# Value products of 64 keys in quarters of the TensorE array, in two PSUM banks, inside the second product

## The chip, the cores and the metric

The kernel runs on one core of a Trainium2 chip. The time is what the device takes for one execution, in microseconds (us). Three runs of the kernel before took 995.18, 995.64 and 997.73 us; their median is 995.64. One further execution was profiled.

## The reference

Sliding-window attention (8 batches, 8 heads, 576 positions, head size 64, window 128, a slope per head) feeds a two-layer network with a squared relu.

```python
scores = scale * np.matmul(q, k.transpose(0, 1, 3, 2))
bias = slopes[:, None, None] * (-np.abs(rel).astype(np.float32))[None, :, :]
mask = (rel >= 0) & (rel < window)
scores = np.where(mask, scores + bias[None], -1000000000.0)
scores = scores - np.max(scores, axis=-1, keepdims=True)
attn = np.exp(scores)
attn = attn / (np.sum(attn, axis=-1, keepdims=True) + 1e-09)
attn_out = np.matmul(attn, v)
x = attn_out.transpose(0, 2, 1, 3).reshape(B * S, H * D)      # 4608 x 512
h = np.maximum(x @ w_in, 0.0)                                 # w_in 512 x 2048
out = h * h @ w_out                                           # w_out 2048 x 512
```

## The kernel before

The 4608 rows are cut into 9 chunks of 512 columns (the data lies transposed: features on partitions, rows along the free axis). For each chunk the network runs 16 steps f. A **first product** (`gemm1`, L169) multiplies 128 columns of w_in with the chunk's attention output: 12 products of 512 columns into the PSUM bank g, four input tiles times three high and low parts. ScalarE's relu (L178) reads g, VectorE squares (L184), ScalarE casts the high part hh (L186), VectorE takes the low part hl (L188). A **second product** (`gemm2`, L199) multiplies w_out with hh and hl of two steps earlier: four output banks acc, three products each. The program alternates first and second products; each is a half step t, first products at even t, second products at odd t.

Attention for the next chunk is put between these products. A chunk has four pairs of heads; a pair has two **segments** of 256 rows, sg 0 and sg 1, and both together form a `Couple`. Every eight half steps there is a **visit** (part 0 in the main loop). It does the value products of the couple before (`both`, which calls `mix`, L335) into the bank at, reads at out to xu (ScalarE's cast L359, VectorE's subtraction L360), loads the q, k and v of the next couple (SP), and makes the score products of a new couple (`Couple.scores`, L414), which write two banks s and the bank g. The scores of segment 1 share g between the two heads j; a GpSimd no-operation lets the second head start only when the first is done there. Then ScalarE copies the scores out (`base`, L441 and L448), VectorE puts the part of the earlier keys in (`fold`, L460 and L464), VectorE and ScalarE make the softmax (L276, L283), GpSimd divides by the sum (`norm`, L294). Three and five half steps behind the visit a `middle` stands ahead of a first product, once for each segment: TensorE transposes the weights (`turn`, L302), ScalarE copies them (L309), GpSimd splits them into `prev` and `own`, the keys of the block before and of the same block, with zeros where a key does not belong (L312, L318).

`mix` multiplies, for each segment, i = 0, 1 and both heads j, 128 keys of `prev` and 128 keys of `own` with v: products of 128 columns in half of the array each (128 rows by 64 columns), accumulated in the bank at.

Each name of a PSUM tile (g, at) has one buffer: g goes from the first product to its relu, and at a visit to the scores and ScalarE's copies of them, and then to the next first product. The order on TensorE is that of the program text in the main loop; on the other engines a scheduler places the instructions by a simulated time line. The start of the program (about 145 us) is ordered by a planner; the change touches it at segment 16 alone.

Of the kernel before, what the change touches and what calls it, by code (L numbers as in the profile page):

```python
# [33 lines left out]
LATER = [("z", 7)]  # L34
RING = lambda k: 55 + 10.5 * (k - 8)
CONV = lambda f: 36 + 6 * f
FIRST = 35
SYNC = mybir.DependencyInfo(mybir.DependencyClass.Sync, mybir.DependencyReason.DATA)
CST = 256 + 128 * H
ENGINES = {e: getattr(mybir.EngineType, e) for e in ("PE", "DVE", "Activation", "Pool", "SP")}  # L40
# [6 lines left out]
class Kern:  # L47
    def __init__(self, ctx, tc, qkd, vd, w1d, w2d, cstd, outd):
        self.tc, self.nc = tc, tc.nc
        self.qkd, self.vd = qkd, vd  # L50
        self.w1d, self.w2d, self.cstd, self.outd = w1d, w2d, cstd, outd
        ep = lambda name, bufs, **kw: ctx.enter_context(tc.tile_pool(name=name, bufs=bufs, **kw))
        self.c = ep("const", 1)
        self.ld = ep("ld", 3)
        self.tp = ep("tp", 3)
        self.pp = ep("pp", 2)
        self.sm = ep("sm", 6)
        self.xu = ep("xu", 8)
        self.hp = ep("hp", 3)
        self.op = ep("op", 4)  # L60
        self.sc = ep("sc", 1, space=PSUM)
        self.at = ep("at", 1, space=PSUM)
        self.g1 = ep("g1", 1, space=PSUM)
        self.ac = ep("ac", 4, space=PSUM)
        self.cst = self.c.tile([128, CST], F32, name="cst")
        self.ident = self.cst[:, 0:128]
        self.mask = self.cst[:, 128:192].bitcast(I32)
        self.never = self.cst[:, 192:256]
        self.raw, self.w = [None] * NF, [None] * NF
        self.nc.alloc_sbuf_tensor("arena", [128, NF * 2048], F32)  # L70
        self.arena = self.nc.sbuf_base - NF * 8192
        self.x, self.qk, self.v, self.h, self.segs = {}, {}, {}, {}, {}
        at = lambda slot, name, shape: self.nc.alloc_sbuf_tensor_at(name, shape, F32, offset=self.arena + slot * 4096).ap()
        self.wide = [at(2 * (NF - 3), "wide", [128, H, 256])[:, 2 * p : 2 * p + 2] for p in range(NP)]
        self.room_t = [at(2 * (NF - 5) + n, f"tw{n}", [128, 4, 256]) for n in range(4)]
        self.start_banks = [self.ac.tile([128, 512], F32, name="acc") for _ in range(4)]
# [111 lines left out]
        nc.vector.tensor_tensor(hl, r, hh.bitcast(F32), op=ALU.subtract)  # L188

    def gemm2(self, c, f):  # L190
        nc = self.nc
        hh, hl = self.h.pop((c, f))
        if f == 0:
            self.acc = self.start_banks if c == 0 else [self.ac.tile([128, 512], F32, name="acc") for _ in range(4)]
        wh, wl = self.w[f][:, 1, :, 1], self.w[f][:, 1, :, 0]
        for m in range(4):
            ms = slice(m * 128, m * 128 + 128)
            for i, (w, h) in enumerate(((wh, hh), (wh, hl), (wl, hh))):
                nc.tensor.matmul(  # L199
                    self.acc[m], w[:, ms], h, start=(f == 0 and i == 0), stop=(f == NF - 1 and i == 2)  # L200
                )
            if f == NF - 1:
                o = self.op.tile([128, 512], F32, name="o")
                out = self.outd[m * 128 : m * 128 + 128, 512 * c : 512 * c + 512]
                if c == NCH - 1 and m == 3:
                    nc.scalar.copy(o[:, 0:256], self.acc[m][:, 0:256])
                    nc.vector.tensor_copy(o[:, 256:512], self.acc[m][:, 256:512])
                    nc.sync.dma_start(out[:, 0:256], o[:, 0:256])
                    nc.scalar.dma_start(out[:, 256:512], o[:, 256:512])
                    continue  # L210
                (nc.scalar.copy if m % 2 else nc.vector.tensor_copy)(o, self.acc[m])
                nc.sync.dma_start(out, o)


class Segment:
# [133 lines left out]

    def both(self, other):
        K = self.K
        X = K.at.tile([128, 512], F32, name="at")
        for s in (self, other):
            s.X = X[:, 256 * s.sg : 256 * s.sg + 256]
            s.mix(s.sg == 0)
        u = K.x[self.c, self.p] = K.xu.tile([128, 2, 512], F32R, name="xu")
        self.nc.scalar.copy(u[:, 0], X)  # L359
        self.nc.vector.tensor_tensor(u[:, 1], X, u[:, 0].bitcast(F32), op=ALU.subtract)  # L360

    def soft(self):
        for m in range(4):
# [12 lines left out]
class Couple:  # L376
# [4 lines left out]

    def __init__(self, K, q):
        self.K, self.nc = K, K.nc
        self.both = [Segment(K, 2 * q), Segment(K, 2 * q + 1)]

    def scores(self):
        K, nc = self.K, self.nc
        self.S = K.sc.tile([128, 2, 512], F32, name="s")  # L390
        self.G = K.g1.tile([128, 512], F32, name="g")
        todo = []
        for h in range(2):
            base, extra = (h, h + 1), (2 - 2 * h,)
            for j in range(2):
                first = [(0, i, p) for i in range(2) for p in ([(0, 1, 2)] if h == 0 else [base, extra])]
                shared, rest = ([(1, i, p) for i in range(2)] for p in (base, extra))
                at = 0
                for s, i, part in shared + first + rest if j == 0 else first + rest + shared:
                    blocks = [x for x in part if x >= self.both[s].late.get(2 * i + h, 0)]  # L400
                    if blocks:
                        to, n = self.spot(s, j, i, part == extra), len(blocks)
                        a = 64 * (blocks[0] - part[0])
                        todo.append((at, h, j, s, i, blocks[0], n, to[64 * h : 64 * h + 64, a : a + 64 * n], s == 1 and part == base))
                        at += 64 * n
        done = None
        qk = K.qk[self.both[0].c, self.both[0].p]
        for at, h, j, s, i, a, n, to, shared in sorted(todo, key=lambda y: y[:3]):
            u, r = 4 * s + 2 * i + h, slice(64 * j, 64 * j + 64)
            q0, k0 = 64 * u + 640 * s, 256 + 64 * (u + a)  # L410
            if shared and j == 1 and done:
                turn = nc.gpsimd.nop()
                K.tc.add_manual_dep(turn.ins, done.ins.name, SYNC, reason="one head at a time in the shared bank")
            mm = nc.tensor.matmul(  # L414
                to, qk[r, q0 : q0 + 64], qk[r, k0 : k0 + 64 * n], start=True, stop=True, skip_group_check=True,
            )
            if shared and j == 0:
                done = mm
            elif shared and done:
                K.tc.add_manual_dep(mm.ins, turn.ins.name, SYNC, reason="one head at a time in the shared bank")  # L420
                done = None
# [173 lines left out]
def start(K):  # L595
# [31 lines left out]
    for k in range(18):  # L627
# [19 lines left out]
        else:  # L647
# [6 lines left out]
                P.add(n("e", m), "Activation", 0.4, (n("t", m),) + ((n("e", m - 1),) if m else ()), d + 0.5, do(G.exp, m))  # L654
            P.add(n("r"), "DVE", 0.4, (n("e", 3),), d + 1, G.sums)
            P.add(n("n"), "Pool", 1.05, (n("r"),), d + 1, G.norm)
            if k > 16:
                continue
            P.add(n("z"), "PE", 0.55, (n("n"),) + chain("z"), d + 1, G.turn, ("at", "pp"), "t")
            P.add(n("o"), "Activation", 0.6, (n("z"),), d + 1, G.out, None, "at")  # L660
            P.add(n("p"), "Pool", 0.72, (n("o"),), d + 1.5, G.before)
            P.add(n("m"), "Pool", 0.66, (n("p"),), d + 1.5, G.same)
            if k > 15:
                continue
            P.add(n("x"), "PE", 1.1, (n("m"), ("v", c, p)) + chain("x"), d + 2, G.values, "at", "pp")
            P.add(n("h"), "Activation", 0.4, (n("x"),), d + 2, G.high)
            P.add(n("l"), "DVE", 0.36, (n("h"),), d + 2, G.low, None, "at")
# [26 lines left out]
@with_exitstack  # L694
def tile_attn_moe(ctx: ExitStack, tc: tile.TileContext, *aps):
    K = Kern(ctx, tc, *aps)
    K.const()
    with tc.manual_schedule(engines={ENGINES["PE"]}):
        with tc.manual_schedule(engines={e for n, e in ENGINES.items() if n != "PE"}):
            start(K)  # L700
        pairs = {8: (K.segs[16], K.segs[17])}
        for n in range(NF, NF * NCH + 2):
            for t in (2 * n, 2 * n + 1):
                q, part = divmod(t - FIRST, 8)
                q += 9
                with tc.high_priority(offset=50):
                    if part == 0:
                        if q - 1 in pairs:
                            first, second = pairs.pop(q - 1)
                            first.both(second)  # L710
                        if q + 1 < 4 * NCH:
                            K.load(*divmod(q + 1, 4))
                        if q < 4 * NCH:
                            C = Couple(K, q)
                            C.front()
                            pairs[q] = C.both
                    if part in (3, 5) and q in pairs:
                        pairs[q][part // 4].middle()
                if t % 2 == 0 and n < NF * NCH:
                    for _ in K.gemm1(*divmod(n, NF)):  # L720
                        pass
                if t % 2:
                    K.gemm2(*divmod(n - 2, NF))


def _consts():
# [47 lines left out]
```

## Time and profile before

| what | us |
|---|---|
| median of three runs | 995.64 |
| the profiled execution | 996.04 |
| its span, first to last instruction | 994.2 |
| TensorE busy, all matrix products | 984.2 |
| first product, L169 | 433.9 |
| second product, L199 with hh and with hl | 388.7 and 227.6 |
| value products, L335 into at | 63.8 |

The profile's page gives the busy time of each engine, then the chain of work that ended last, then groups of instructions with their idle time and what ended it. In its rows PE is TensorE's products, PEld its weight loads, DVE is VectorE, ACT ScalarE, POOL GpSimd, SP SyncE. A row of a group reads: line, engine, operation, output<-input, shapes, count, busy time and mean duration. A group's busy time counts the overlap of products in different parts of the array once; rows of the chain show what TensorE spends on a piece from end to end. The kernel's products of fp32 data leave two records each in the trace.

### The profile page before, as it was taken

The page shows a single profiled execution, that of the slowest core. Times are in us where ns is not written, and L with a number is a line of the kernel's source. Part 1 is how long each engine was busy: PE and PEld are TensorE (multiplying, and loading weights), DVE is VectorE, ACT ScalarE, POOL GpSimd, SP SyncE. Part 2 cuts the span into 40 slices and gives each one's busy share as a digit, 9 for nine tenths or more (in the row PEclk, how much of TensorE's full clock was granted, in tenths as well). Part 3 has the DMA queues.
Part 4 walks back from the last instruction along what each step waited for, and adds up shares of the span by engine and source line. Part 5 has one row for each costly group of instructions (what it writes and reads, how often), then busy time and mean ns, then how long its engine had stood idle before and what let it go on. Part 6 is the DMA issues. An engine that isn't in the chain of part 4 may idle for free.

```text
span 994.2 us, 16896 instructions
## 1 busy us (share of the span) xinstructions
PE 984.2 (99%) x6545; PEld 814.1 (82%) x6548; DVE 438.4 (44%) x1269; ACT 453.7 (46%) x1180; POOL 191.8 (19%) x252
## 2 busy tenths in 40 slices
PE   9899999999999999999999999999999999999998
PEld 5678788888888888888888888888888888888886
DVE  6889824444443434344444344333434444422222
ACT  7899744444433444344444343334444444422221
POOL 4132321221112222222212211122222221100000
PEclk9999999999999999999999999999999999999999
DMA  9971202111211002111211121110111110001001
GB/s 350 404 276 53 63 14 80 38 39 38 80 38 39 26 20 73 39 38 38 81 38 38 38 80 38 38 39 19 65 35 39 38 57 1 1 1 43 1 1 42
DMA packets 26943, 61.50 MB, mean 62 GB/s; under 512 B 2928, under 2 KB 4336, under 8 KB 26864
## 3 DMA queue, kind: packets, MB, share of 16 engines
q1 hardware_dynamic: 26432, 59.91, 17.4%
q8 instruction: 51, 0.84, 0.3%
q10 hardware_dynamic: 432, 0.52, 0.2%
q14 instruction: 28, 0.23, 0.1%
HBM read 50.99 MB, written 9.44 MB: 61 GB/s over the span
## 4 chain that ended last, share of the span: by engine, by line
PE 97%; DVE 1%; ACT 1%; issue 0%; POOL 0%; DVEq 0%; POOLq 0%; ACTq 0%
PE acc L199 41%; PE g L169 40%; PE at L335 6%; PE at L302 3%; PE s L414 2%; PE g L414 2%; PE g L105 1%; PE s L239 1%; PE acc L335 1%; PE at L530 0%; PE s L498 0%; PE acc L498 0%; PE acc L533 0%; DVE tw L508 0%; ACT w L155 0%
## 5 line engine op out<-in xcount | busy, mean ns | idle before, releaser
L169 PE MATMUL g<-xu,w 128*128 128x512 f32 x1728 | 433.9, 400 | 2.6 <-ACT r L178 2.6
L199 PE MATMUL acc<-hh,w 128*128 128x512 f32 x1152 | 388.7, 398 | 0.0
L169 PEld LDWEIGHTS g<-xu,w 128*128 128x128 f32 x1728 | 333.3, 196 | 65.3 <-ACT r L178 3.3
L199 PEld LDWEIGHTS acc<-hh,w 128*128 128x128 f32 x1152 | 224.8, 195 | 46.1 <-issue 1.5
L184 DVE TENSOR_TENSOR r<-r 128x512 f32<-128x512 f32 x128 | 88.6, 692 | 342.3 <-ACT r L178 340.4
L199 PE MATMUL acc<-hl,w 128*128 128x512 f32 x576 | 227.6, 395 | 0.0
L178 ACT ACTIVATE r<-g 128x512 f32<-128x512 f32 x144 | 85.5, 594 | 299.5 <-PE g L169 299.2
L188 DVE TENSOR_TENSOR hl<-r,hh 128x512 fp32r<-128x512 f32 x144 | 102.2, 710 | 108.9 <-ACT hh L186 104.7
L186 ACT CAST hh<-r 128x512 fp32r<-128x512 f32 x144 | 89.2, 619 | 95.0 <-DVE r L184 94.5
L199 PEld LDWEIGHTS acc<-hl,w 128*128 128x128 f32 x576 | 112.5, 195 | 20.4
L294 POOL TENSOR_TENSOR t<-t,nm 128x512 f32<-128x512 f32 x64 | 81.1, 1267 | 239.2 <-DVE nm L291 214.2
L283 ACT ACTIVATE t<-t,nm 128x128 f32<-128x128 f32 x256 | 99.5, 390 | 35.2 <-DVE nm L276 35.0
L312 POOL TENSOR_SCALAR_AFFINE_SELECT pp<-pp 128x512 f32<-128x512 f32 x64 | 43.4, 679 | 185.7 <-ACT pp L309 185.6
L335 PEld LDWEIGHTS at<-pp,v 128*64 128x64 f32 x1024 | 55.2, 137 | 12.7 <-issue 12.0
L335 PE MATMUL at<-pp,v 128*64 128x128 f32 x1024 | 63.8, 276 | 0.0
L309 ACT COPY pp<-at 128x512 f32<-128x512 f32 x72 | 42.1, 584 | 45.5 <-PE at L302 44.5
L276 DVE CUSTOM_DVE_ANT_0 t<-t,cst 128x128 f32<-128x128 f32 x256 | 59.2, 293 | 1.0
L450 POOL MEMSET t<- 64x128 f32 (+1 forms) x35 | 8.1, 232 | 236.3 <-PE g L414 235.9
L460 DVE COPY_PREDICATED t<-cst,s 64x256 f32<-64x256 int32 x85 | 37.8, 445 | 32.4 <-ACT t L448 19.1
L283 ACT ACTIVATION_READ_ACCUMULATOR t<-t,nm 128x1 f32 x256 | 48.0, 187 | 0.0
L318 POOL TENSOR_SCALAR_AFFINE_SELECT pp<-pp 128x512 f32<-128x512 f32 x64 | 42.3, 661 | 4.4
L414 PE MATMUL s<-qk 64*64 64x64 f32 (+2 forms) x988 | 40.2, 253 | 0.0
(71 smaller groups left out, 587.4 us busy)
## 6 DMA issues: line engine op xcount, KB each, us to landing
raw<-in_dram SPq DMA_DIRECT2D x32, 512.0 KB, 8.9
qk<-in_dram SPq DMA_DIRECT2D x32, 320.0 KB, 3.5
v<-in_dram SPq DMA_DIRECT2D x32, 320.0 KB, 3.0
qk<-in_dram SPq DMA_DIRECT2D x38, 256.0 KB, 3.8
out_dram<-o SPq DMA_DIRECT2D x35, 256.0 KB, 2.7
v<-in_dram SPq DMA_DIRECT2D x3, 256.0 KB, 5.0
wide<-in_dram SPq DMA_DIRECT2D x3, 256.0 KB, 5.2
qk__200<-in_dram SPq DMA_DIRECT2D x2, 256.0 KB, 5.6
```

The costliest lines, as they stand in the source:

```text
L169: nc.tensor.matmul(g, w[:, cc * 128 : cc * 128 + 128], xs[cc][:, part], start=i == 0, stop=i == 11)
L178: nc.scalar.activation(r, g, AF.Relu)
L184: nc.vector.tensor_tensor(r, r, r, op=ALU.mult)
L186: nc.scalar.copy(hh, r)
L188: nc.vector.tensor_tensor(hl, r, hh.bitcast(F32), op=ALU.subtract)
L199: nc.tensor.matmul(self.acc[m], w[:, ms], h, start=(f == 0 and i == 0), stop=(f == NF - 1 and i == 2))
L276: self.nc.vector.tensor_tensor_reduce(self.t[:, m], self.t[:, m], self.K.nrel(2 * self.p + m // 2), -0.125, BIG, ALU.add, ALU.min, self.nm ...
L283: self.nc.scalar.activation(self.t[:, m], self.t[:, m], AF.Exp, bias=nm[:, m : m + 1], scale=-1.0, accum_out=nm[:, 4 + m : 5 + m],)
L294: self.nc.gpsimd.tensor_tensor(self.t, self.t, self.nm[:, 8:12].unsqueeze(2).to_broadcast([128, 4, 128]), op=ALU.mult)
L312: self.nc.gpsimd.affine_select(self.prev, self.own, pattern=[[0, 4], [-1, 128]], compare_op=ALU.is_gt, fill=0.0, base=0, channel_multiplier=1,
L335: self.nc.tensor.matmul(self.X[r, o : o + 128], v[:, 2 * sg + k, r], src[:, j], start=start and n == 0, stop=n == 3 - self.skip, skip_grou ...
L414: mm = nc.tensor.matmul(to, qk[r, q0 : q0 + 64], qk[r, k0 : k0 + 64 * n], start=True, stop=True, skip_group_check=True,)
```

## The change

`quarters` takes the place of `mix` in a visit. It cuts the 128 keys in halves of 64, each in one row half of the array, and with the two heads j in the two column halves each product uses a quarter. The first half of the keys accumulates in the bank at, the second half in the bank g (a tile of g is made ahead of the values, and the scores of the same visit use it afterwards). In each block half of the queries are left out where the weights are zero, so that half of the products have 64 columns. The two banks are added when they are read out: VectorE copies segment 0's half of g and ScalarE segment 1's to an SBUF tile, VectorE adds at to it, and the cast and the subtraction read the sum. The score products of head j = 1 come first in g, those of j = 0 wait for them. `gemm2` is a generator now, and a visit stands behind the first three of its twelve products. FIRST goes from 35 to 37, so that visits stand a step later against the chunks, and the middle of segment 16 goes from the start to the steady part.

```diff
-FIRST = 35
+FIRST = 37
...
     def gemm2(self, c, f):
+        for _ in self.gemm2_parts(c, f):
+            pass
+
+    def gemm2_parts(self, c, f):
...
+            yield
...
-    def both(self, other):
-        K = self.K
+    def quarters(self, X):
+        K, sg = self.K, self.sg
+        v = K.v[self.c, self.p]
+        own, prev = (a.rearrange("p (j i) c -> p j i c", j=2) for a in (self.own, self.prev))
+        for i in range(2):
+            for full in (True, False):
+                for half in range(2):
+                    src, k = (own, 1) if full == (half == 0) else (prev, 0)
+                    a, e = (0, 128) if full else (64 * half, 64 * half + 64)
+                    r = slice(64 * half, 64 * half + 64)
+                    for j in range(2):
+                        d = slice(64 * j, 64 * j + 64)
+                        self.nc.tensor.matmul(
+                            X[half][d, 128 * i + a : 128 * i + e], v[r, 2 * sg + i + k, d], src[r, j, i, a:e],
+                            start=sg == 0 and i == 0 and full, stop=True, skip_group_check=True,
+                        )
+
+    def both(self, other, G):
+        K, nc = self.K, self.nc
         X = K.at.tile([128, 512], F32, name="at")
+        u = K.x[self.c, self.p] = K.xu.tile([128, 2, 512], F32R, name="xu")
         for s in (self, other):
-            s.X = X[:, 256 * s.sg : 256 * s.sg + 256]
-            s.mix(s.sg == 0)
-        u = K.x[self.c, self.p] = K.xu.tile([128, 2, 512], F32R, name="xu")
-        self.nc.scalar.copy(u[:, 0], X)
-        self.nc.vector.tensor_tensor(u[:, 1], X, u[:, 0].bitcast(F32), op=ALU.subtract)
+            a = 256 * (1 - s.sg)
+            s.X = X[:, 256 * s.sg : 256 * s.sg + 256], G[:, a : a + 256]
+            s.quarters(s.X)
+        low = K.op.tile([128, 512], F32, name="o")
+        for s in (self, other):
+            (nc.scalar.copy if s.sg else nc.vector.tensor_copy)(low[:, 256 * s.sg : 256 * s.sg + 256], s.X[1])
+        nc.vector.tensor_tensor(low, X, low, op=ALU.add)
+        nc.scalar.copy(u[:, 0], low)
+        nc.vector.tensor_tensor(u[:, 1], low, u[:, 0].bitcast(F32), op=ALU.subtract)
...
-                for s, i, part in shared + first + rest if j == 0 else first + rest + shared:
+                for s, i, part in rest[:1] + shared + first + rest[1:] if j == 1 else first + rest + shared:
...
-                if t % 2:
-                    K.gemm2(*divmod(n - 2, NF))
+                if t % 2 == 0:
+                    continue
+                parts = K.gemm2_parts(*divmod(n - 2, NF))
+                next(parts)
+                with tc.high_priority(offset=50):
+                    if part == 0 and q - 1 in pairs:
+                        first, second = pairs.pop(q - 1)
+                        G = K.g1.tile([128, 512], F32, name="g")
+                        first.both(second, G)
...
+                for _ in parts:
+                    pass
```

On TensorE, before, this stood at a visit in the middle of the program (the name in brackets is the engine or queue whose semaphore the instruction waits for): the last products of a first product, the value products, and the first of the scores.

```order
L169 MATMUL g<-xu,w_479 128x512 x11
L335 MATMUL at<-pp,v 64x128 [waits DMAHW3_49,PE_49,Pool_49]
L335 MATMUL at<-pp,v 64x128 x3
L335 MATMUL at<-pp,v 64x128 [waits Pool_49]
L335 MATMUL at<-pp,v 64x128 x3
L335 MATMUL at<-pp,v 64x128 [waits Pool_49]
L335 MATMUL at<-pp,v 64x128 x3
L335 MATMUL at<-pp,v 64x128 [waits Pool_49]
L335 MATMUL at<-pp,v 64x128 x3
L414 MATMUL g<-qk 64x64 [waits DMAHW5_49,DMAHW4_49,Activation_49]
L414 MATMUL s<-qk 64x192
```

The first score product into g waited for ScalarE's relu of the first product above it. Now, on TensorE, the start of the values at a visit:

```order
L169 MATMUL g<-xu,w_530 128x512 x11
L203 MATMUL acc<-hh,w_445 128x512
L203 MATMUL acc<-hl,w_445 128x512 [waits DVE_49]
L203 MATMUL acc<-hh,w_445 128x512
L369 MATMUL at<-pp,v 64x128 [waits DMAHW3_49,PE_49,Pool_49]
L369 MATMUL at<-pp,v 64x128
L369 MATMUL g<-pp,v 64x128 [waits Activation_49]
L369 MATMUL g<-pp,v 64x128
```

It is the third value product that waits for the relu, behind three products of the second product. And, on TensorE, the end of the values with the first scores of the same visit:

```order
L369 MATMUL g<-pp,v 64x64 x2
L440 MATMUL s<-qk 64x192 [waits DMAHW4_49]
L440 MATMUL s<-qk 64x64 [waits DMAHW5_49]
L440 MATMUL s<-qk 64x128
L440 MATMUL s<-qk 64x64
L440 MATMUL g<-qk 64x64 [waits Activation_49]
L440 MATMUL g<-qk 64x128 x2
L440 MATMUL s<-qk 64x64
```

The fifth score product, the first into g, now waits for ScalarE at the count that the copy of g (L384) raises; four products into s stand ahead of it, one for each quarter. On VectorE, now, around the read-out of one visit:

```order
L188 TENSOR_TENSOR hl<-r,hh 128x512 [waits PE_49,Activation_49]
L384 COPY o<-g 128x256 [waits DMAHW3_49,PE_49]
L385 TENSOR_TENSOR o<-at,o 128x512 [waits Activation_49]
L387 TENSOR_TENSOR xu<-o,xu 128x512 [waits Activation_49]
L486 COPY_PREDICATED t<-cst,s 64x4x64 [waits PE_49,Activation_49,Pool_49]
```

The copy and the addition are new, and stand behind hl of the step's first product; the copy waits for TensorE at the count of the last value product, and the subtraction into xu has moved behind them. On ScalarE, now, at the same visit:

```order
L178 ACTIVATE r<-g 128x512 [waits DVE_49,PE_49]
L186 CAST hh<-r 128x512 [waits DVE_49]
L384 COPY o<-g 128x256 [waits DMAHW3_49,DVE_49]
L386 CAST xu<-o 128x512 [waits DVE_49]
L474 COPY t<-g 128x2x128 [waits PE_49]
L474 COPY t<-g 64x2x128
```

The copy of g is new here; it waits for VectorE at the count that VectorE's copy of g raises. The cast to xu has moved behind the addition.

More of the change, by code (lines that the diff above doesn't have):

```diff
@@ L209, in gemm2 @@
                     nc.scalar.dma_start(out[:, 256:512], o[:, 256:512])
-                    continue
-                (nc.scalar.copy if m % 2 else nc.vector.tensor_copy)(o, self.acc[m])
-                nc.sync.dma_start(out, o)
+                else:
+                    (nc.scalar.copy if m % 2 else nc.vector.tensor_copy)(o, self.acc[m])
+                    nc.sync.dma_start(out, o)
+            yield
 class Segment:
@@ L376, with __init__ @@
 class Couple:
-    def __init__(self, K, q):
-        self.K, self.nc = K, K.nc
+    def __init__(self, K, q, G):
+        self.K, self.nc, self.G = K, K.nc, G
         self.both = [Segment(K, 2 * q), Segment(K, 2 * q + 1)]
@@ L390, in scores @@
         self.S = K.sc.tile([128, 2, 512], F32, name="s")
-        self.G = K.g1.tile([128, 512], F32, name="g")
         todo = []
@@ L410, in scores @@
             q0, k0 = 64 * u + 640 * s, 256 + 64 * (u + a)
-            if shared and j == 1 and done:
+            if shared and j == 0 and done:
                 turn = nc.gpsimd.nop()
@@ L416, in scores @@
             )
-            if shared and j == 0:
+            if shared and j == 1:
                 done = mm
@@ L656, in start @@
             P.add(n("n"), "Pool", 1.05, (n("r"),), d + 1, G.norm)
-            if k > 16:
+            if k > 15:
                 continue
@@ L662, in start @@
             P.add(n("m"), "Pool", 0.66, (n("p"),), d + 1.5, G.same)
-            if k > 15:
-                continue
             P.add(n("x"), "PE", 1.1, (n("m"), ("v", c, p)) + chain("x"), d + 2, G.values, "at", "pp")
@@ L706, in tile_attn_moe @@
                 with tc.high_priority(offset=50):
[L707 to L716, printed above, removed]
                     if part in (3, 5) and q in pairs:
@@ L721, in tile_attn_moe @@
                         pass
-                if t % 2:
-                    K.gemm2(*divmod(n - 2, NF))
+                if t % 2 == 0:
[7 more added lines that the diff above has]
+                        first.both(second, G)
+                        if q + 1 < 4 * NCH:
+                            K.load(*divmod(q + 1, 4))
+                        if q < 4 * NCH:
+                            C = Couple(K, q, G)
+                            C.front()
+                            pairs[q] = C.both
+                for _ in parts:
+                    pass
 def _consts():
```

## The prediction

> **What bounds the kernel now.** I read the page first: busy shares, then the chain that ended last.
>
> ```profile
> span 994.2 us, 16896 instructions
> PE 984.2 (99%) x6545; PEld 814.1 (82%) x6548; DVE 438.4 (44%) x1269; ACT 453.7 (46%) x1180; POOL 191.8 (19%) x252
> PE 97%; DVE 1%; ACT 1%; issue 0%; POOL 0%; DVEq 0%; POOLq 0%; ACTq 0%
> ```
>
> TensorE works 984.2 of 994.2 us and holds 97% of the chain. A microsecond taken off TensorE is a microsecond off the kernel, and a microsecond for which TensorE waits is added in full. The other engines matter only where TensorE waits for them. Second view: the chain in order of time around one visit (start, duration, what).
>
> ```profile
> 500.16 2.80 PE g L169 x12
> 502.96 1.90 PE at L335 x32
> 504.85 0.21 PE g L414
> ...
> 506.21 0.01 PE g L414
> 506.22 3.00 PE acc L199 x12
> 509.21 2.80 PE g L169 x12
> 512.01 2.80 PE acc L199 x12
> ```
>
> The visit stands between a first product (L169) and a second product (L199): value products 1.90 us, score products from 504.85 to 506.22, so 1.37, and the second product takes 3.00 where it takes 2.80 elsewhere: 0.20 for the change of shape. Nothing idles. From the end of the first product (502.96) to the start of the next (509.21) pass 6.25 us. Third view: the score products alone, in 27 windows, one around each visit (TensorE busy, count of records); the first row is this visit, the second the sum.
>
> ```profile
> 502.70:506.90 4.20, 1.43 (x52) 1.30 (x52) 1.00 0.21 54
> sum 113.50, PE 41.17 PEld 36.67; mean PE 1.52 PEld 1.36
> L360 DVE TENSOR_TENSOR xu<-at,xu 128x512 fp32r<-128x512 f32 x28 | 19.3, 690 | 0.4
> ```
>
> This visit's 1.43 busy is 1.37 on the chain (the last ends overlap), so the mean of 1.52 is about **1.46**, and a mean visit takes 1.90 + 1.46 + 3.00 = 6.36. The third row counts 28 visits; one of them, the last, has no scores behind its values.
>
> **The change part by part.** *Value products in quarters.* They took 1.90 for 16 products of 128 columns in each half of the array. Now each quarter gets 768 columns, where the score products, also in quarters, had about 672 (2688 over four) and took 1.37 to 1.46. So about 1.5 us, bounded by 1.4 (at the best rate of the scores, one change of shape less) and 1.7. Gain 0.2 to 0.5 a visit, if nothing else is late.
>
> *The place inside the second product.* Three of its twelve products now run ahead of the values: 3 x 2.80/12 = 0.70, so the values start at about 503.66. They now also write g, which ScalarE is reading until then.
>
> *What g needs next.* In the order of before g went from the first product to the scores. Now it goes first product, values, scores, next first product. I read ScalarE's and VectorE's timeline of the same visit (start, duration, instruction):
>
> ```profile
> 502.99 0.60 ACT L178 ACTIVATE r<-g 128x512 f32<-128x512 f32 x1 [3.62 <-PE g L169]
> 504.35 0.62 ACT L186 CAST hh<-r 128x512 fp32r<-128x512 f32 x1 [0.76 <-DVE r L184]
> 504.90 0.59 ACT L359 CAST xu<-at 128x512 fp32r<-128x512 f32 x1
> 506.26 1.31 ACT L448 COPY t<-g 64x256 f32<-64x256 f32 x4 [0.77 <-PE g L414]
> 505.00 0.69 DVE L188 TENSOR_TENSOR hl<-r,hh 128x512 fp32r<-128x512 f32 x1 [0.68 <-ACT hh L186]
> ```
>
> The relu leaves g at 503.59, ahead of 503.66: the 0.70 covers it, with 0.07 to spare less a handover of about 0.04, so I cost it at nothing (bounds 0 and 0.1). The values end near 505.2. Then both halves of g are copied out before the scores may write there. In the order of the built program TensorE's fifth score product (the first into g) waits for ScalarE's copy; ScalarE's copy waits for VectorE's copy; VectorE's copy waits for the last value product and stands behind hl. hl ends at 505.69, after the values, so hl sets the start. The durations of such copies, and that two engines copy halves of one bank one after the other, stand at the end of the program:
>
> ```profile
> 990.49 0.37 ACT L206 COPY o<-acc 128x256 f32<-128x256 f32 x1 [0.81 <-PE acc L199]
> 990.89 0.42 DVE L207 COPY o<-acc 128x256 f32<-128x256 f32 x1 [0.41 <-ACT o L206]
> ```
>
> VectorE could have begun with ScalarE, and began 0.03 after its end. So: hl ends 505.69, +0.03, VectorE 0.42 to 506.14, +0.03, ScalarE 0.37 to 506.54, +0.04 for TensorE. **The first score into g starts at 506.58**, 3.62 after the first product's end. The handover of 0.04 is from the one long wait of TensorE in the trace:
>
> ```profile
> 40.70 0.61 ACT r L178
> 41.30 0.04 issue
> 41.35 4.62 PE g L169 x12
> ```
>
> *What is left behind the wait.* All later products queue behind the waiting one, the rest of the second product too. Ahead of it stand four products, one a quarter; the two quarters that write g have done 64 of about 672 columns. So 0.90 of the stage remains: 0.90 x 1.46 = 1.31. The handover between heads through GpSimd, already there, now has five products behind the last g product of the first head instead of ten: 0 to 0.2 more, I take 0.05, since the other quarters still have work. After that the nine products left: 3.00 - 0.70 = 2.30.
>
> Sum for a mean visit: 3.62 + 1.36 + 2.30 = 7.28 against 6.36: **+0.92**. Bounds: 0.85 (no handover cost) and 1.2 (0.2 there, 0.1 at the restart). The 0.4 won in the values is lost, since hl and the two copies end 1.4 later than the values do. 27 x 0.92 = 24.8; the 28th visit waits for no copy and gains 0.4.
>
> *More instructions off the path.* Each visit adds on VectorE a copy (0.42) and an addition (0.69 as the L360 row), on ScalarE a copy (0.37). They end near 505.69 + 0.85 + 0.03 + 0.69 + 0.03 + 0.59, so 507.9 with ScalarE's cast, about when the scores end (507.8): no delay of its own; without that cover up to 0.1. The next first product needs g read out: 1.31 for the four copies gives about 509.3, and it starts near 510.2. Still covered. But the chain from scores to softmax to turn has lost 0.70, since the scores end later in the second product. The tightest visit (GpSimd's norm, then TensorE's turn, which needs it):
>
> ```profile
> 299.19 1.04 POOL L294 TENSOR_TENSOR t<-t,nm 128x512 f32<-128x512 f32 x1 [7.34 <-DVE nm L291]
> 300.29 0.66 PE L302 MATMUL at<-cst,t 128*128 128x128 f32 x4
> ```
>
> 300.23 to 300.29: 0.06 of slack. There 0.64 becomes a wait. The four visits of that chunk have the same form: 4 x 0.64 = 2.6 (bounds 0, if the copies of acc which no longer fall into a visit give it back, and 5, if a second chunk falls short). The turn of segment 16 leaves the start for the steady part: the same four transposes on TensorE either way: 0. The four output copies stand two half steps ahead of a visit now instead of beside it: 0. SP's loads keep their place in the visit: 0.
>
> Total: 24.8 + 2.6 - 0.4 = **+27 us**. The profiled execution took 996.04 (span 994.2 and 1.84 around it), within 0.4 of the median 995.64. So **1023 us**; with the bounds, 1017 to 1034.
>
> **The rivals.** *A, faster:* VectorE's copy of the first segment's half runs while the second segment's products run, so the scores never wait. The price then is 0.70 + 1.5 + 1.46 + 2.30 = 5.96 against 6.36, 27 x -0.40 - 0.4 + 2.6 for the turns: 987 us. For it: the copy reads only that half, and its products end near 504.5. It decides from the point where the copy starts before hl (505.00). Against: it stands behind hl, and waits for the last value product. Chance 0.09.
>
> *B, slower by less:* both halves are copied at once. The wait ends 0.40 earlier: 27 x 0.40 = 10.8 less, 1012 us. Against it: 990.49 and 990.89 above. Chance 0.07. [...]
>
> *C, the clock falls:* TensorE stands idle some 1.1 us in every visit. The twelve products after the one wait of 2.64 us took 4.62 instead of 2.80, at a lower granted clock:
>
> ```profile
> 38.40:41.30 2.90, 0.31 (x2) 0.00 (x0) 2.82 (x4) 2.85 (x3) 0.00 (x0) 1.00 1.02 404
> 43.00:46.00 3.00, 3.00 (x12) 1.98 (x14) 2.98 (x11) 1.75 (x2) 0.00 (x0) 0.55 1.03 409
> ```
>
> If a visit did that, 27 x 1.8 = 49 more: 1072 us. The first row is the wait (0.31 busy of 2.90), the second the clock behind it (0.55). A visit is idle less than half as long. Chance 0.05. [...]
>
> *D, the change does not do what it says:* the four quarters do not run side by side. Values then take 2.8, end at 506.5, and each visit is 0.8 longer still: 1045. Against it: the scores' 1.37 in quarters. Chance 0.03. *E:* the shorter slack of 0.70 makes turns or relus late in more chunks: 5 to 15 us more, 1028 to 1038. Chance 0.04.
>
> **How the numbers follow.** My forecast has 0.72. The range 1011 to 1036 takes in its bounds, B and half of E: about 0.8. A change of 0.3% (3 us) is about what a measurement of this kernel can tell from none. Faster is A: 0.09. Within it lies only a mixture of A and B, to which I give 0.02 of B's 0.07. Slower is the rest: 0.89.
>
> **What would show it.** In each visit TensorE stands idle about 1.1 us ahead of a score into g, released by ScalarE's copy; VectorE's copy begins at hl's end, ScalarE's behind it; the values take 1.4 to 1.7. The way from one first product to the next across a visit is 7.2 to 7.4. Waits at the turn of 0.6 in one chunk. I am wrong if TensorE's busy share stays at 99%, if the first score into g starts less than 3.2 us after the first product ends, or if the granted clock falls in the visits.

## The result, and the profile after

The changed kernel takes **1024.96 us** (median of four runs, 1024.86 to 1025.1) against 995.61 for the kernel before beside it (995.18 to 997.73): ratio 1.0291, 95% interval 1.0273 to 1.0308, 29.35 us slower. The profiled execution took 1025.1, its span is 1023.4.

The page of the changed kernel: span, busy shares, and the share of each engine in the chain that ended last.

```profile
span 1023.4 us, 18767 instructions
PE 982.4 (96%) x7444; PEld 807.6 (79%) x7444; DVE 467.8 (46%) x1325; ACT 466.8 (46%) x1208; POOL 192.5 (19%) x252
PE 86%; ACT 6%; DVE 4%; issue 3%; POOL 0%; ACTq 0%; DVEq 0%; POOLq 0%
```

TensorE has hardly less to do than before (982.4 against 984.2 us), but the span is 29.2 longer: TensorE now waits. Its share of the chain falls from 97% to 86%, and ScalarE, VectorE and the gaps between instructions ("issue") hold the rest. What it waits for stands in the view of waits of TensorE (line of the waiting products, what released them; us in total, times, longest):

```profile
PE g L440 <- ACT o L384: 30.4, 27, 1.2
PE g L169 <- ACT r L178: 2.6, 1, 2.6
PE at L307 <- POOL t L299: 1.8, 4, 0.5
```

The first row is new: 27 times, once in each visit with scores, the score products into g wait for ScalarE's copy of g, 30.4 / 27 = 1.13 us each time. The second was there before, at the start of the program. The third is new too: four turns wait for GpSimd's norm. The chain in order of time around one visit (start, duration, what) shows what stands inside the 1.13:

```profile
494.57 2.81 PE g L169 x12
497.39 0.02 issue
497.41 0.61 ACT r L178
498.02 0.02 issue
498.04 0.70 DVE r L184
498.74 0.02 issue
498.77 0.63 ACT hh L186
499.39 0.02 issue
499.42 0.04 DVE hl L188
499.45 0.57 issue
500.02 0.43 DVE o L384
500.45 0.02 issue
500.48 0.38 ACT o L384
500.86 0.04 issue
500.90 0.29 PE g L440 x2
...
502.23 2.30 PE acc L203 x9
504.53 2.80 PE g L169 x12
```

From 497.39 to 500.90 the path leaves TensorE altogether: relu, square, hh and hl of the first product just done, then VectorE's copy, then ScalarE's copy. Before, those four steps ran beside the visit and nothing waited for them. The same stretch on the engines' timelines (start, duration, instruction, and in brackets the idle time before it and what ended it):

```profile
498.00 0.33 PE L369 MATMUL at<-pp,v 64*64 64x128 f32 x2
498.06 0.33 PE L369 MATMUL g<-pp,v 64*64 64x128 f32 x2
499.39 0.33 PE L440 MATMUL s<-qk 64*64 64x192 f32 x1
499.40 0.22 PE L369 MATMUL g<-pp,v 64*64 64x64 f32 x1
499.42 0.69 DVE L188 TENSOR_TENSOR hl<-r,hh 128x512 fp32r<-128x512 f32 x1 [0.68 <-ACT hh L186]
500.02 0.42 DVE L384 COPY o<-g 128x256 f32<-128x256 f32 x1
500.48 0.37 ACT L384 COPY o<-g 128x256 f32<-128x256 f32 x1 [1.09 <-DVE o L384]
500.90 0.33 PE L440 MATMUL g<-qk 64*64 64x64 f32 x2 [1.02 <-ACT o L384]
```

The values start at 498.00 and the scores at 499.39: 1.39 us for the values, where they took 1.90. The last value is done at 499.40 + 0.22 = 499.62. VectorE is in hl by then (499.42) and takes its copy only behind it, with no idle time in brackets (the records of one engine overlap a little at their ends: 500.02 is 0.09 before hl's record ends). ScalarE was idle for 1.09 and was released by VectorE's copy, not by TensorE.

A reading of the records of all 27 such visits, each from the end of the last record of its first product: values start at 0.63 and end at 2.24; hl's record ends at 2.74 and VectorE's copy starts at 2.65 (7 visits) or 2.77 (20); the first score into g starts at 3.62 in the mean (3.53 to 3.65). To the next first product it is 7.235 in the mean, and 6.185 in the kernel before. I call this last number the **way**; the chain's rows give about 0.15 more for either kernel. The visit shown above is the shortest of the 27 (its way is 7.00). The way grows by 1.05, and 27 x 1.05 = 28.4 is nearly all of the loss.

### The profile page after: what moved, and what is told of

It is laid out like the page before. It is cut to its first block, busy times and chain, and to the rows that moved or that the text cites. A ratio compares the mean times of both kernels' runs of the same rounds, so it can differ in the third digit from the quotient of the medians.

```text
span 1023.4 us, 18767 instructions
## 1 busy us (share of the span) xinstructions
PE 982.4 (96%) x7444; PEld 807.6 (79%) x7444; DVE 467.8 (46%) x1325; ACT 466.8 (46%) x1208; POOL 192.5 (19%) x252
## 4 chain that ended last, share of the span: by engine, by line
PE 86%; ACT 6%; DVE 4%; issue 3%; POOL 0%; ACTq 0%; DVEq 0%; POOLq 0%
PE g L169 38%; PE acc L203 36%; PE at L307 3%; PE g L440 2%; PE s L440 2%; DVE r L184 2%; ACT r L178 2%; ACT hh L186 2%; DVE o L384 1%; ACT o L384 1%; PE g L105 1%; PE at L340 1%; ACT t L288 1%; PE s L244 1%; ACT t L474 1%
## 5 line engine op out<-in xcount | busy, mean ns | idle before, releaser
L203 PE MATMUL acc<-hh,w 128*128 128x512 f32 x1152 | 393.0, 398 | 0.0
L288 ACT ACTIVATE t<-t,nm 128x128 f32<-128x128 f32 x256 | 99.6, 391 | 38.8 <-DVE nm L281 38.7
L317 POOL TENSOR_SCALAR_AFFINE_SELECT pp<-pp 128x512 f32<-128x512 f32 x64 | 44.3, 692 | 178.5 <-ACT pp L314 178.5
L440 PE MATMUL g<-qk 64*64 64x128 f32 (+1 forms) x400 | 35.4, 273 | 30.4 <-ACT o L384 30.4
L440 PEld LDWEIGHTS g<-qk 64*64 64x64 f32 x400 | 23.2, 132 | 40.0 <-ACT o L384 37.7
L440 PE MATMUL s<-qk 64*64 64x64 f32 (+2 forms) x988 | 51.9, 255 | 0.0
L288 ACT ACTIVATION_READ_ACCUMULATOR t<-t,nm 128x1 f32 x256 | 48.2, 188 | 0.0
L369 PEld LDWEIGHTS at<-pp,v 64*64 64x64 f32 x896 | 39.7, 134 | 10.1 <-issue 10.1
```

The source lines that it names most:

```text
L203: nc.tensor.matmul(self.acc[m], w[:, ms], h, start=(f == 0 and i == 0), stop=(f == NF - 1 and i == 2))
L288: self.nc.scalar.activation(self.t[:, m], self.t[:, m], AF.Exp, bias=nm[:, m : m + 1], scale=-1.0, accum_out=nm[:, 4 + m : 5 + m],)
L317: self.nc.gpsimd.affine_select(self.prev, self.own, pattern=[[0, 4], [-1, 128]], compare_op=ALU.is_gt, fill=0.0, base=0, channel_multiplier=1,
L440: mm = nc.tensor.matmul(to, qk[r, q0 : q0 + 64], qk[r, k0 : k0 + 64 * n], start=True, stop=True, skip_group_check=True,)
```

## The experiments

My theory: the time is lost because g can be handed to the scores only after hl, VectorE's copy and ScalarE's copy, one behind the other. Rivals: the place of the visit (inside the second product, nearer to the turns) costs much of it; or the quarters themselves do. Each ratio below is against runs of the kernel before beside it: median 994.93 in the first four experiments, 995.93 in the last three.

**One copy instead of two.** Both halves of g are copied by ScalarE at once, and nothing waits for VectorE. The values of the two segments change places in g, so that the one copy finds them in the order of the output.

```diff
-            a = 256 * (1 - s.sg)
+            a = 256 * s.sg
...
-        for s in (self, other):
-            (nc.scalar.copy if s.sg else nc.vector.tensor_copy)(low[:, 256 * s.sg : 256 * s.sg + 256], s.X[1])
+        nc.scalar.copy(low, G)
```

> ScalarE copies both halves of g at once, VectorE copies nothing, so hl and one handover are no longer ahead of the scores into g. Theory 1 (the loss is the chain hl, VectorE's copy, ScalarE's copy): the copy starts at the values' end, about 2.3 us after the first product's end, takes 0.59 and frees g at 2.9 instead of 3.6: 0.7 less in 27 visits, 19 us, 1006 us. Theory 2 (the loss is the place inside the second product): no change, 1025. Theory 3 (the loss is any copy of g at all, however many): about 1025 less one copy of 0.4, 1014.

Measured: 1006.56 us, ratio 1.0115 (1.01 to 1.013). Waits of TensorE, then ScalarE's timeline in one visit:

```profile
PE g L439 <- ACT o L383: 11.8, 27, 0.5
PE at L307 <- POOL t L299: 2.1, 4, 0.5
```
```profile
492.67 0.58 ACT L383 COPY o<-g 128x512 f32<-128x512 f32 x1 [0.28 <-PE g L369]
```

The copy of the whole bank takes 0.58, less than the two halves one behind the other (0.42 + 0.37), and TensorE's last value now releases it, not VectorE. It starts 2.29 after the first product, and 0.69 a visit is gone: the way is 6.54. So of the 1.05, about 0.45 was VectorE standing in hl (the read-out starts at 2.29 instead of 2.74) and 0.24 the second copy with its handover (the read-out takes 0.58 instead of 0.83). This split is read from the two traces; no run changes one of the two alone. 0.36 stays: the read-out of g still lies between values and scores.

**The place alone.** The value products, cast and subtraction are those of before, without quarters and copies; the visit stays inside the second product, with the new order of the scores.

```diff
-            a = 256 * (1 - s.sg)
-            s.X = X[:, 256 * s.sg : 256 * s.sg + 256], G[:, a : a + 256]
-            s.quarters(s.X)
-        low = K.op.tile([128, 512], F32, name="o")
-        for s in (self, other):
-            (nc.scalar.copy if s.sg else nc.vector.tensor_copy)(low[:, 256 * s.sg : 256 * s.sg + 256], s.X[1])
-        nc.vector.tensor_tensor(low, X, low, op=ALU.add)
-        nc.scalar.copy(u[:, 0], low)
-        nc.vector.tensor_tensor(u[:, 1], low, u[:, 0].bitcast(F32), op=ALU.subtract)
+            s.X = X[:, 256 * s.sg : 256 * s.sg + 256]
+            s.mix(s.sg == 0)
+        nc.scalar.copy(u[:, 0], X)
+        nc.vector.tensor_tensor(u[:, 1], X, u[:, 0].bitcast(F32), op=ALU.subtract)
```

> The visit stays inside the second product, but the value products are those of before, in halves of the array and in the bank at alone. Theory 1: g is free when the relu has read it, no wait at the scores; the way across a visit is that of before (0.63 + 1.90 + 1.46 + 2.21 = 6.2), the turns of one chunk still wait, 1.8 to 2.6 us in all: 997 to 999 us. Theory 2: most of the 29 us stay, above 1015.

Measured: 1001.32 us, ratio 1.0057 (1.0042 to 1.0072), some 2 to 4 us above what I expected. No score waits; the four turns wait as in the changed kernel (2.1 us). The way is 6.296, 0.11 longer than before, though nothing waits in the visit. The next run asks where that comes from.

**The place alone, with the old order of the scores.** As the last one, and the scores' order of before.

```diff
-                for s, i, part in rest[:1] + shared + first + rest[1:] if j == 1 else first + rest + shared:
+                for s, i, part in shared + first + rest if j == 0 else first + rest + shared:
...
-            if shared and j == 0 and done:
+            if shared and j == 1 and done:
...
-            if shared and j == 1:
+            if shared and j == 0:
```

> The visit inside the second product with the value products of before, as in the run of the place alone, and the score products in the order of before too (head 0 first in g). If the 0.1 that a visit took there beyond the way of before is the order of the scores (a handover between heads with less work beside it): 27 x 0.11 = 3 less than that run, 998 us. If it is the place: 1001, no change.

Measured: 998.35 us (10 runs), ratio 1.0023 (1.0012 to 1.0034). The way is 6.187, that of before: the place costs nothing on the way, and the new score order costs 0.11 a visit. (The medians of the two runs are 3 us apart, and the executions of this one lie between 996.74 and 1002.06; the ways in the two traces are the firmer evidence.) What the place costs stands in the turns:

```profile
PE at L307 <- POOL t L299: 2.0, 4, 0.5
```

**The visit back ahead of the second product**, with quarters and copies.

```diff
-                next(parts)
```

> Quarters as in the change, but the visit stands ahead of the second product again. Theory 1: the score into g still starts 3.6 us after the first product's end, since hl sets that, and all 12 products (2.9) are behind the scores instead of 9 (2.2): 0.7 more in 27 visits, 19 us, 1044 us. Theory 2 (the place costs): faster than 1025, towards 1000.

Measured: 1043.09 us, ratio 1.0477 (1.0462 to 1.0493). Waits of TensorE:

```profile
PE g L440 <- ACT o L384: 33.0, 27, 1.3
PE g L369 <- ACT r L178: 9.0, 28, 0.3
```

The values now wait for the relu as well (9.0 / 28 = 0.32), because no product of the second product stands ahead of them. The values end 2.24 and the first score into g starts 3.62 after the first product, both as in the changed kernel, so leading with the values wins nothing. The way is 7.93, or 0.70 longer: just the three products that no longer run ahead of the wait.

**No copies.** The addition and the two copies go; quarters, order and place stay. What the products add up in g is left out of the output.

```diff
-        low = K.op.tile([128, 512], F32, name="o")
-        for s in (self, other):
-            (nc.scalar.copy if s.sg else nc.vector.tensor_copy)(low[:, 256 * s.sg : 256 * s.sg + 256], s.X[1])
-        nc.vector.tensor_tensor(low, X, low, op=ALU.add)
-        nc.scalar.copy(u[:, 0], low)
-        nc.vector.tensor_tensor(u[:, 1], low, u[:, 0].bitcast(F32), op=ALU.subtract)
+        nc.scalar.copy(u[:, 0], X)
+        nc.vector.tensor_tensor(u[:, 1], X, u[:, 0].bitcast(F32), op=ALU.subtract)
```

> Quarters and place as in the change, but the half in g is neither copied out nor added: the values of half of the keys are left out of the output. Theory 1: no wait at the scores, way across a visit 0.63 + 1.39 + 1.4 + 2.2 = 5.6 against 7.2 now and 6.2 before, 27 x 1.6 = 43 less than the change: 981 to 984 us. If the quarters themselves cost something, or the place does: above 995.

Measured: 983.22 us, ratio 0.9881 (0.9864 to 0.9897). The way falls to 5.76, and TensorE is at 99% again:

```profile
PE 970.0 (99%) x7441; PEld 803.6 (82%) x7444; DVE 439.1 (45%) x1269; ACT 455.4 (46%) x1180; POOL 192.4 (20%) x252
```

So the quarters do what they are meant to: beside the run of the place alone (6.296) the way is 0.53 shorter. Most of it comes from the columns left out: the 32 records of the values before are 16 products, 8 in each half of the array, so 1024 columns a half; a quarter now gets 768, and 1.90 x 768/1024 = 1.43, where 1.39 was measured. That is an estimate, as no run has quarters with all the columns. All of the 0.53, and 0.94 more, is paid for reading the second bank out.

**Scores further back.** One copy, the old score order, and three more products of the second product between values and scores, so that they cover the copy. The new lines of the main loop:

```diff
...
                         first.both(second, G)
+                    next(parts)
+                    with tc.high_priority(offset=50):
```

> One copy of g by ScalarE, and three products of the second product between the values and the scores, so that TensorE works while g is copied; the scores in the order of before. Theory 1: the values end at 2.0, the three products at 2.8, g is free at 2.9; no wait of note, way across a visit 2.9 + 1.45 + 1.6 = 5.95 to 6.0 against 6.2 before. But the scores end 1.4 later in the second product than before, so the turns of many visits wait for GpSimd's norm, 9 to 12 us in all: 996 to 1001 us. If turns do not wait: 989.

Measured: 1010.87 us, ratio 1.0148 (1.0134 to 1.0162), a miss by 10 us and more. The way came out at 6.056, and no score waits. But the scores end later, and so do softmax and norm, and the turns wait for them:

```profile
PE at L307 <- POOL t L299: 16.0, 17, 1.8
```

17 turns now wait, up to 1.8 us, where the change has four: the term that I had sized too small (9 to 12 us in all, against 18.8 in the table below). The slack between the scores and the turn is a second limit right behind the first.

**Turns later too.** As the last one, and the middles stand at parts 5 and 7 instead of 3 and 5.

```diff
-                    if part in (3, 5) and q in pairs:
-                        pairs[q][part // 4].middle()
+                    if part in (5, 7) and q in pairs:
+                        pairs[q][part // 6].middle()
```

> As the run with the scores behind six products, but the turns stand two half steps later, five and seven behind the visit. Theory 1: the turns no longer wait, 27 x 0.2 less than before and 0.4 at the last visit: 988 to 991 us. If later turns make the value products of the next visit wait for GpSimd: above 995.

Measured: 994.1 us (7 runs, 992.39 to 994.93) against 995.93, ratio 0.9975 (0.9964 to 0.9986): 0.25% faster than the kernel before, and 3% faster than the change. The executions of the kernel before lie further apart among themselves (994.57 to 997.38), so a gain as small as this rests on the medians and the interval. I had expected 988 to 991, a gain larger by 3 us or more. Waits of TensorE, then two pieces of the chain: a wait at 172 us, and what stands behind the values of a visit:

```profile
PE g L169 <- ACT r L178: 4.6, 4, 2.6
```
```profile
171.96 0.09 ACT t L288
172.06 0.02 issue
172.08 0.61 ACT r L178
172.69 0.04 issue
172.73 1.44 PE g L169 x5
...
483.34 0.91 PE acc L203 x3
484.24 0.21 PE g L439
...
485.61 1.61 PE acc L203 x6
487.22 2.85 PE g L169 x12
```

No turn waits. Three first products now wait for a relu (4.6 less the 2.6 of the start, 2.0 in all); in the one shown the relu (172.08) stands behind an exponential of the softmax (L288) on ScalarE. And the three products between values and scores take 0.91 instead of 0.70, so about 0.2 of the quarters' 0.5 goes to the second change of shape.

The runs can be added up from two readings of each trace: the way, and the pauses before the turns, from the start of the product before a turn to the turn's start, less the 0.23 that this is without a wait. In the kernel before these pauses add up to 0.2 us, in the changed kernel to 2.5, where the waits view counts 1.8; the column gives what is more than in the kernel before.

| kernel | way | 27 x (way - 6.185) | pauses more | last visit | sum | measured over its before |
|---|---|---|---|---|---|---|
| the change | 7.235 | +28.4 | +2.3 | -0.4 | +30.3 | +29.4 |
| one copy | 6.542 | +9.6 | +2.5 | -0.4 | +11.7 | +11.6 |
| place alone | 6.296 | +3.0 | +2.5 | 0 | +5.5 | +6.4 |
| place alone, old order | 6.187 | +0.1 | +2.4 | 0 | +2.5 | +2.4 |
| visit ahead | 7.934 | +47.2 | -0.2 | +0.4 | +47.4 | +48.2 |
| no copies | 5.762 | -11.4 | +2.1 | -0.4 | -9.7 | -11.7 |
| scores later | 6.056 | -3.5 | +18.8 | -0.4 | +14.9 | +14.9 |
| turns later | 6.056 | -3.5 | +1.8 (2.0 of it relus) | -0.4 | -2.1 | -1.8 |

Two terms and the last visit carry every run within 1 us, but for the one without copies, whose other 2 us I did not trace.

## Why the prediction was right, point by point

The forecast was 1023 us, and its mechanism held; 2 us are missing. That it came so close is in part luck: the terms in the table add up to +30.3 where the prediction has +27, and 0.9 of these 3.3 do not show in the measured time, for a reason that I did not trace.

- *First score into g at 3.62 after the first product:* 3.62 in the mean. The order of it held link by link: hl, VectorE's copy, ScalarE's copy, TensorE. That the two copies and not the values set it is shown by the run with one copy: its values end at 2.24 too, and the score starts at 2.93.
- *Values in quarters 1.5, and without effect on the sum:* the working reads as if each half of the array had 16 products before; it is 16 in all, 8 in each half. Measured: 1.39, even below my lower bound of 1.4, and without effect as long as the copies stand.
- *Relu covered by three products:* g's first value starts 0.06 behind at's, at the place that the order gives it anyway. Without the cover (the visit ahead) TensorE was idle there for 0.32 a visit, and the values, which began 0.70 earlier, ended no earlier.
- *The visit +0.92:* measured +1.05, and two terms of it were mis-sized. First, **what is left of the scores behind the wait**: I had 0.90 x 1.46 + 0.05 = 1.36, and it takes 1.41. The new order makes the whole score stage 1.56 long where it was 1.46 (the two runs of the place alone: 0.11 a visit apart); 0.90 x 1.56 = 1.40. My 0.05 for the handover between the heads was half of the 0.11 that the new order costs. Second, **the visit of before**: I added up chain pieces end to end, 1.90 for the values. In the records the scores of before begin 1.83 after the first product, 0.07 before the last value record ends. A wait takes this overlap away too. The second product is 0.09 to 0.10 shorter in the records than in the chain's rows on both sides of the subtraction, and cancels. So 0.05 + 0.07 is the difference, 27 x 0.12 = 3.2 us.
- *Four turns wait 0.64 each, 2.6 in all:* pauses of 0.55 to 0.69, 2.5 in all, in one chunk, as said. The last visit gives back 0.38 (said 0.4).
- *Rivals.* A (the copy overlaps) falls: VectorE's copy starts at hl's end in all 27 visits, from 0.08 before the end of its record to 0.03 behind it, and at least 0.4 behind the last value. B (both copies at once) falls: ScalarE's copy starts 0.03 to 0.04 after VectorE's ends, each time. What keeps ScalarE back is a semaphore of the program, as the order of the built program shows (ScalarE's L384 waits for VectorE's count); what the chip would do with both copies at once, no run shows. One engine for the whole bank was 18 us faster than two engines with half each, but only 0.24 of the 0.69 a visit are the halves one behind the other; the rest is hl. C (the clock) falls, by these rows of the changed kernel (window, length, busy time and count of TensorE, weight loads, VectorE, ScalarE, GpSimd, then granted clock, DMA share, GB/s):

```profile
500.00:501.00 1.00, 0.10 (x4) 0.10 (x8) 0.56 (x3) 0.37 (x1) 0.00 (x0) 1.00 0.33 79
160.00:890.00 730.00, 699.05 (x5778) 581.18 (x5776) 314.71 (x947) 309.88 (x847) 141.93 (x190) 1.00 0.13 40
```

In the first window TensorE works 0.10 of 1.00 us, and in the second lie 26 of the 27 waits: the granted clock is 1.00 in both. C's premise, too, was weaker than I took it for: the same long wait at the start stands in all nine profiles, and in three of them the clock did not fall (see the last section). D (quarters one after the other) falls with 1.39. E (more turns late) falls for the change itself, with four turns, and came true in the experiment that moved the scores further back.

## What to carry to other kernels

When a stage on the busiest engine is made shorter by writing into a buffer that other work hands on, first follow that buffer: here 0.5 us of products was saved a visit and 1.5 us of read-out came between two users of one bank. Count from the moment the reading engine is free, not from the moment the data are there, and give the read-out of one bank to one engine, the one that has nothing queued (here one copy in place of two was 18 us faster, and 0.45 of its 0.69 us a visit was the queue). Before work is moved later to hide such a wait, look up the slack of everything behind it: here 0.06 us stood between GpSimd and the turn, and the wait moved there.

## What the runs showed of the hardware that was not expected

- Products in quarters run on into the next stage. In the timeline above the first score (499.39, into s) starts while records of the last values (499.40, into g, until 499.62) are still running in other quarters, so no gap shows between values and scores, both being quarters. Changes between full products and quarters do cost: in the run with the turns later, 0.91 instead of 0.70 for three products with a change on either side.
- TensorE stood idle for about 1.1 us every 28 us, 27 times, and the granted clock stayed at 1.00. The one wait of 2.6 to 2.7 us at the start stands in all nine profiles: in six a stage at 0.50 follows it (mean granted clock of the profiled execution 0.997 or 0.998), in three (the visit ahead, no copies, the place alone with the old order) the clock stays at 1.00, so its length alone does not decide. The slow stage lasts 3.41 us (42.31 to 45.72 in the kernel before, 41.66 to 45.07 in the changed kernel; about twice as long in the run with one copy, whose mean is 0.997). What decides whether it comes, no run shows.
- The order of the score products alone, with the same products, was worth 0.11 us a visit (6.296 against 6.187). Why the head j = 1 first takes longer I read as the handover through GpSimd with less work beside it; it was not tried apart.
